# Moving the expert-part table comparisons from VectorE to GpSimd, with the row-0 cases gathered in a tile of their own

## The chip, the cores and the metric

The kernel runs on one core of a Trainium2 chip. The metric is the device time of one execution in microseconds (us), lower is better. The engines are TensorE (PE; its weight loads are PEld), VectorE (DVE), ScalarE (ACT), GpSimd (POOL) and SyncE (SP), which here only issues DMAs.

## The reference

Two layers act on the same normalised input and are added to it (S = 2048 tokens, D = 512):

```python
xn = _layernorm(x, axis=-1)
return x + _A_ref(xn, dft_seq_re, dft_seq_im, dft_hid_re, dft_hid_im) + _B_ref(xn, w_q, k1, k2, u, v)
# A: y = Cr @ (xn @ Wr.T) - Ci @ (xn @ Wi.T)          (2048x2048 and 512x512 matrices)
# B: 32 heads; two score sets against 64 keys, the best 2 of each, the best 2 of the 4 sums,
#    softmax over these, then sum over heads and both picks of g * gelu(xn . u[e]) * v[e], 4096 experts
```

The Fourier matrices of A are inputs like any other. The kernel computes A with the symmetries that a Fourier matrix has, from a part of each matrix, and so has to find out whether the matrices that it was given have those symmetries. If one does not, a slower path at the end recomputes A.

## The kernel before, in words

**Stages.** Up to about 80 us the Fourier part of A is done. Up to about 440 us the scores of the 32 heads are computed in eight groups of four heads, and each token's two experts per head are chosen (the routing). The rest, from about 440 us, is the expert part: 14 blocks of 128 tokens run densely over all 4096 experts on TensorE, and the last two blocks (`NS = 2`) run sparsely, by fetching the rows of u and v that their tokens picked.

**A block of the expert part** has 16 steps: eight `v_part` steps (a product with v into the accumulator `pv`, lines 1018 to 1025) and eight `u_part` steps for the block two ahead (lines 947 to 961). In between, `g_mm` builds one-hot matrices on VectorE (L980, L988, L991) and multiplies them on TensorE (L993), `w_part` forms the weights (L1004 on VectorE, L1011 on ScalarE, L1014 on VectorE), and `finish` evicts `pv` with the VectorE instruction L1038. That instruction frees a PSUM buffer which the next `u_part` steps need.

**The sparse rows** run beside the dense blocks. `fetch` gathers one row per token with an indirect DMA from GpSimd (L1049) into one of five `ga` buffers; `dot` multiplies on VectorE (L1065); `gain` scales on ScalarE (L1075, L1076, L1078) and adds into `ov` on GpSimd (L1083), after which the next row is fetched. There are 128 such rounds.

**The comparisons.** `compare(n)` (lines 720 to 788) tests one 128x1024 piece of the sequence matrices, n from 0 to 63: `ri` (real or imaginary) is n // 32, the column group `g` is n // 8 % 4, and `kk` is n % 8. Its two DMAs from SP (L731 from `ca`, 128 rows of 512 bytes, and L732 from `cb`, 128 rows of 3584 bytes) fill a tile `cx`. `diff` replaces three of its four sections by differences (or sums) to the first and folds the first onto itself (`mirror`); `judge` sums the absolute values on ScalarE (L778 what should be zero, L780 the rest). For g = 0 row 0 of the tile has rules of its own, so `diff` uses L739, L741 (twice, with the mask `not0`), L743 and a second `mirror` on row 0 alone; for other groups one or two tensor_tensor instructions (L752) do it. 28 pieces (`EARLY`, 8 to 23 and 40 to 51) are compared in the routing stage, on GpSimd. The other 36 (0 to 7, 24 to 39, 52 to 63) are compared in the expert part, where `at` is None and `v_eng` is VectorE. `compare_w` (lines 1108 to 1144) does the same for the hidden-dimension matrices, on VectorE, in four more units.

**Order.** `paced` hands out one unit of two streams at every step, the `fit` units at even steps and the compare units at odd ones, spread over 12 blocks. `after(2, f)` puts the work two steps later, and the judging two steps after that, and `hold` ties these to the step's last matmul in the scheduler's order. Each engine runs its instructions in the order in which they stand. The tiles of `compare`, of `fit` (512 KB weight pieces read by ScalarE, L1150 and L1151) and of `w_part` share one tag of `WB = 4` buffers, so a load waits until the buffer's last reader is done. All loads named here stand in SP's one queue, with those of the token blocks (L939, L944), of the rows to be added (L1031) and the stores (L1039).

Of the kernel before, what the change touches and what calls it, by code (L numbers as in the profile page):

```python
# [8 lines left out]
F32 = mybir.dt.float32  # L9
# [6 lines left out]
AF = mybir.ActivationFunctionType  # L16
# [3 lines left out]
P = 128  # L20
# [16 lines left out]
def tile_fnet_peer(ctx, tc, x, ca, cb, c5, wt, wf, wr, wq, kt, ut, vn, uv, out):  # L37
# [57 lines left out]
    sums_sb = cst.tile([P, 138 + NF + 3], F32, name="sums")  # L95
    chk, asum = sums_sb[:, 0:70], sums_sb[:, 70:138]
# [5 lines left out]
    fits = sums_sb[:, 138:]  # L102
# [453 lines left out]
    def part_b(safe, stS, stP, stE, xt, u_sb, cmp_p):  # L556
# [163 lines left out]
        def compare(n, at=None):  # L720
# [10 lines left out]
            nc.sync.dma_start(tf[:, :P], ca[ri, g, :, kk * P:(kk + 1) * P])  # L731
            nc.sync.dma_start(tf[:, P:], cb[ri, g, kk].rearrange("p b c -> p (b c)"))  # L732
            sgn = (((1, 1, 1), (-1, 1, -1)), ((-1, -1, 1), (1, -1, -1)))[ri][odd]
            ops = [ALU.subtract if v > 0 else ALU.add for v in sgn]
            op = ops[1]

            def diff():
                if g == 0:
                    nc.vector.tensor_tensor(tv[:, 1], tv[:, 1], tv[:, 0], op=ops[0])  # L739
                    for i in (2, 3):  # L740
                        nc.vector.scalar_tensor_tensor(tv[:, i], tv[:, 0], not0, tv[:, i], op0=ALU.mult, op1=ops[i - 1])  # L741
                    f = (-1 if ri else 1) * sgn[1] * sgn[2]
                    nc.vector.tensor_tensor(tv[0:1, 3], tv[0:1, 3], tv[0:1, 2],  # L743
                                            op=ALU.subtract if f > 0 else ALU.add)
                else:
                    sets = {}
                    for i, o in enumerate(ops):
                        sets.setdefault(o, []).append(i + 1)
                    for o, ix in sets.items():
                        sl = slice(ix[0], ix[-1] + 1, ix[1] - ix[0] if len(ix) > 1 else 1)  # L750
                        v = tv[:, sl]
                        v_eng.tensor_tensor(v, v, tv[:, 0:1].to_broadcast([P, len(ix), 256]), op=o)  # L752
                m = ALU.add if ri else ALU.subtract

                def mirror(v):

                    c = 0 if kk else 1
                    v_eng.tensor_tensor(v[:, 2:4, c:], v[:, 2:4, c:], v[:, 0:2, c:], op=m)  # L758
# [3 lines left out]
                if g == 0:  # L762
# [332 lines left out]
        def pick(after, k=1):  # L1095
            done[0] += k
            made = nc.cur_bb.bb.instructions
            for f in picks[done[1]:-(-len(picks) * done[0] // turns)]:
# [3 lines left out]
                for i in made[first:]:  # L1102
                    if i.engine in (mybir.EngineType.DVE, mybir.EngineType.Activation):
                        follow(i, after)
                    if i.engine == mybir.EngineType.Activation and after.ins.name in GL:
                        follow(i, GL[after.ins.name])

        def compare_w(n):


# [24 lines left out]
                nc.vector.memset(r[:, 255:256], 0.0)  # L1135
            nc.vector.scalar_tensor_tensor(v[2], v[0], not0, v[2], op0=ALU.mult, op1=op)
            if ri:
                nc.scalar.activation(v[0][0:1, 0:P], v[0][0:1, 0:P], AF.Abs, accum_out=chk[0:1, 68 + half:69 + half])
# [5 lines left out]
            after(2, lambda: nc.scalar.activation(f, f, AF.Abs, accum_out=chk[:, n:n + 1]))  # L1144

        def fit(n):

# [14 lines left out]
        def verdict():  # L1162
# [1 line left out]


            N = NF + 3
            fm = sums_sb[:, 138 + NF:]
# [3 lines left out]
            cols = ((slice(0, 64), 50), (slice(64, 70), 47))  # L1171
            for i, (c, k) in enumerate(cols):
                nc.vector.tensor_reduce(fa[:, i:i + 1], asum[:, c.start:min(c.stop, 68)], axis=AX.X, op=ALU.add)
# [6 lines left out]
            k = nc.gpsimd.partition_all_reduce(fr[:, 2:], sums_sb[:, 138:], P, bass_isa.ReduceOp.absmax)  # L1180
# [21 lines left out]
            NW + k, *range(2 * k, min(2 * k + 2, NW)), NW + 16 + k)]  # L1202
        todo_n = [n for n in range(68) if n not in EARLY]
        units = [lambda n=n: (compare if n < 64 else compare_w)(n) for n in todo_n]
        streams = [[fit_units, 0, 0], [units, 0, 0]]

        def flush(mm):
# [11 lines left out]
                st[2] += 1  # L1219

        if not safe:
            nc.vector.memset(chk[:, 68:70], 0.0)
# [237 lines left out]
```

## Time and profile before

| what | value |
|---|---|
| median of 3 runs | 1119.79 us (1116.18 to 1124.1) |
| the profiled execution | 1113.87 us |
| its span, first to last instruction | 1112.1 us |
| busy share of the span | PE 96%, DVE 90%, ACT 65%, POOL 58% |
| DMA traffic | 196.72 MB, mean 177 GB/s |
| mean granted TensorE clock | 0.987 of full speed |

The profiled execution is 5.9 us below the median of the runs. In the views quoted below, a waiting row reads "engine, line, tile waited <- who released it: us in total, times, longest us"; a group row reads "line engine operation out<-in shapes xcount | busy us, mean ns of one | idle time before it and what ended it"; a timeline row begins with start and duration in us; a row of the windows view gives a stretch, its length, each engine's busy us (and its instructions), the granted clock, the mean busy share of the 16 DMA engines and their GB/s.

### The profile page before, as it was taken

Reading aid. Unit: us, or ns where it says so; the run is one execution under the profiler, and the core shown is the slowest. Engines: PE = TensorE matmul, PEld = TensorE weight load, DVE = VectorE, ACT = ScalarE, POOL = GpSimd, SP = SyncE. Lnnn points to the kernel's source line nnn. Section 1 sums busy time; section 2 is a strip of 40 time slices with the busy share of each in tenths; the row PEclk is TensorE's granted clock in tenths of the full one; section 3 lists DMA queues with packets and bytes.
Section 4 is the critical chain, followed back from the end, with each engine's and each line's share of the span. In section 5 each row is a group of like instructions: output and inputs, shape, how many; then the busy total and the mean of one; then the engine's idle time right before and its main releaser. Section 6 shows DMA issues by size and latency. Waiting matters only on the chain. (4 is left out here: it accounts for less than half of the span.)

```text
span 1112.1 us, 28462 instructions
## 1 busy us (share of the span) xinstructions
PE 1070.3 (96%) x11070; PEld 700.6 (63%) x11070; DVE 996.7 (90%) x2786; ACT 717.7 (65%) x1324; POOL 640.3 (58%) x552
## 2 busy tenths in 40 slices
PE   5899999999999999999999999999998999999897
PEld 4355555454544544987695776968667686786853
DVE  6978897978999999987999999999999999998981
ACT  3576657778788767423766667767566666765660
POOL 0013537588797855211668677756666667667651
PEclk9899999999999999999999999999998999999899
DMA  8248153535446332553677577676767567776521
GB/s 326 83 172 284 49 198 113 173 125 198 153 153 206 106 114 65 186 158 109 186 213 238 193 212 231 225 232 201 215 199 209 182 214 237 230 222 189 158 67 51
DMA packets 84433, 196.72 MB, mean 177 GB/s; under 512 B 10294, under 2 KB 27069, under 8 KB 84288
## 3 DMA queue, kind: packets, MB, share of 16 engines
q1 hardware_dynamic: 63394, 123.49, 33.1%
q0 software_dynamic: 20736, 71.31, 21.8%
q8 instruction: 88, 1.44, 0.5%
q14 instruction: 57, 0.47, 0.1%
q10 hardware_dynamic: 158, 0.01, 0.0%
HBM read 177.68 MB, written 17.10 MB: 175 GB/s over the span
## 5 line engine op out<-in xcount | busy, mean ns | idle before, releaser
L796 PE MATMUL s<-m,xq 128*128 128x512 f16 x1536 | 338.9, 379 | 0.0
L956 PE MATMUL z<-xb,u 128*128 128x128 f16 x5376 | 313.9, 221 | 15.5 <-DVE y L1038 15.5
L956 PEld LDWEIGHTS <-u 128*128 128x128 f16 x5376 | 307.6, 99 | 19.2 <-issue 16.4
L1083 POOL TENSOR_TENSOR ov<-ov,ga 128x512 f32<-128x512 f32 x128 | 203.5, 1590 | 167.2 <-ACT ga L1078 145.7
L1023 PE MATMUL v<-v,act 128*128 128x512 f16 x1344 | 298.6, 379 | 0.0
L796 PEld LDWEIGHTS <-xq 128*128 128x128 f16 x1536 | 148.3, 98 | 171.4 <-issue 0.2
L1023 PEld LDWEIGHTS <-act 128*128 128x128 f16 x1344 | 128.3, 98 | 146.1
L1049 POOL DMA_INDIRECT ga<-in_uv_dram,eix x128 | 173.0, 1351 | 47.2 <-POOL ov L1083 34.2
L980 DVE TENSOR_TENSOR L<-io_lam,cmp 128x2048 f16<-128x2048 f16 x112 | 157.8, 1441 | 13.5 <-PE g L993 13.5
L804 DVE MAX8 vals<-ss 128x8 f32<-128x64 f32 x1024 | 152.4, 216 | 14.1 <-ACT ss L801 14.0
L959 ACT ACTIVATE act<-z,scl 128x512 f32<-128x512 f32 x112 | 75.8, 679 | 97.2 <-PE z L956 96.3
L808 DVE FIND_INDEX8 idx<-vals,ss 128x8 uint16<-128x256 f32 x256 | 107.1, 418 | 0.0
L801 ACT ACTIVATE ss<-s,wsc 128x512 f32<-128x512 f32 x112 | 75.5, 680 | 43.4 <-PE s L796 33.7
L1011 ACT ACTIVATE act<-w 128x1024 f16<-128x1024 f32 x56 | 75.5, 1348 | 43.3 <-DVE w L1004 39.8
L1078 ACT ACTIVATE ga<-ga,za 128x512 f32<-128x512 f32 x128 | 92.1, 721 | 9.8 <-ACT za L1076 0.4
L1014 DVE TENSOR_TENSOR act<-w,act 128x1024 f16<-128x1024 f32 x56 | 86.1, 1539 | 6.7 <-ACT act L1011 5.8
L778 ACT ACTIVATE cx<-cx 128x896 f32<-128x896 f32 x64 | 60.6, 946 | 40.3 <-DVE cx L758 12.9
L1065 DVE SCALAR_TENSOR_TENSOR ga<-ga,px 128x512 f32<-128x512 f32 x128 | 85.6, 676 | 0.1
L1004 DVE SCALAR_TENSOR_TENSOR w<-act,scl,g 128x1024 f32<-128x1024 f32 x56 | 70.9, 1271 | 0.4 <-ACT act L959 0.2
L169 POOL TENSOR_TENSOR wq<-wq,wh 128x1024 f16<-128x1024 f32 x26 | 55.4, 2134 | 24.4 <-ACT wq L166 23.7
L993 PEld LDWEIGHTS <-L 128*128 128x128 f16 x1792 | 52.2, 96 | 9.5 <-issue 2.7
L993 PE MATMUL g<-R,L 128*128 128x32 f16 x1792 | 54.0, 176 | 2.2 <-DVE w L1004 1.9
(274 smaller groups left out, 1312.4 us busy)
## 6 DMA issues: line engine op xcount, KB each, us to landing
cx<-in_cb_dram SPq DMA_DIRECT2D x64, 448.0 KB, 4.6
wq<-in_wq_dram SPq DMA_DIRECT2D x32, 512.0 KB, 5.8
fit<-in_wq_dram SPq DMA_DIRECT2D x28, 512.0 KB, 5.4
uv<-in_ut_dram SPq DMA_DIRECT2D x16, 512.0 KB, 4.1
uv<-in_vn_dram SPq DMA_DIRECT2D x16, 512.0 KB, 3.5
xq<-in_x_dram SPq DMA_DIRECT2D x8, 512.0 KB
xt_d<-xq SPq DMA_DIRECT2D x16, 256.0 KB, 3.0
cx<-in_ca_dram SPq DMA_DIRECT2D x64, 64.0 KB, 2.8
```

The source lines that it names most:

```text
L796: mm = nc.tensor.matmul(ps, xt[i][:, l, kd, :], m[:, r, kd, :], start=(n == 0), stop=(n == 3 * KD - 1))
L804: nc.vector.max(vals[:, i, w, :, h], s[:, g, :])
L808: nc.vector.max_index(idx[:, i, w].rearrange("p k h -> p (k h)"), vals[:, i, w, 0:2].rearrange("p k h -> p (k h)"), s[:, w * HC:g + 1, :]. ...
L956: mm = nc.tensor.matmul(p[:, cc * P:(cc + 1) * P], ug[:, l, c % 2, kd, :], xb[:, r, kd, :], start=(n == 0), stop=(n == 3 * KD - 1))
L980: nc.vector.tensor_tensor(L.rearrange("p t (l two) -> p t l two", two=2), io_lam.rearrange("p (l two) -> p l two", two=2).unsqueeze(1).to_ ...
L993: i = nc.tensor.matmul(p[:, hf, t * NC:(t + 1) * NC], L[:, t, :], R[:, hf * 16 + t, :], start=True, stop=True)
L1014: nc.vector.tensor_tensor(w16[..., 1], w, w16[..., 0], op=ALU.subtract)
L1023: mm = nc.tensor.matmul(pv, w16[:, c, :, l], vg[:, r, c % 2, :], start=(c == 0 and k == 0), stop=(c == NC - 1 and k == 2))
L1049: nc.gpsimd.indirect_dma_start(out=t, out_offset=None, in_=uv, in_offset=bass.IndirectOffsetOnAxis(ap=eix[:, n].rearrange("p k h -> p (k h ...
L1065: nc.vector.scalar_tensor_tensor(t, t, 1.0, T["x"], op0=ALU.mult, op1=ALU.mult, accum_out=T["z", n][:, s:s + 1])
L1078: nc.scalar.activation(t, t, AF.Copy, scale=z)
L1083: T["a"] = nc.gpsimd.tensor_tensor(o, o, t, op=ALU.add)
```

## The change

All compares of the expert part but two (n = 0 and 32, that is g = 0 with kk = 0) run on GpSimd. For the 14 others with g = 0 the rules for row 0 are taken out: rows 1 to 127 are loaded as before, and row 0 of the tile is filled with row 1 once more, by DMAs of one row, so that the form of the other groups serves. Row 0 of these 14 pieces goes into one extra tile `cx_r` (new function `compare_r`): three or four rows in each of four partition quadrants, one class of signs each, compared on VectorE and summed by one ScalarE instruction. The tile is cleared on GpSimd before its eight DMAs. `compare_r` is put in as the third unit of the compare stream, which then has 41 units, and the column sums get one column more.

```diff
-            v_eng = nc.vector if at is None else nc.gpsimd
+            v_eng = nc.vector if n % 32 == 0 else nc.gpsimd
...
-            nc.sync.dma_start(tf[:, :P], ca[ri, g, :, kk * P:(kk + 1) * P])
-            nc.sync.dma_start(tf[:, P:], cb[ri, g, kk].rearrange("p b c -> p (b c)"))
+            own = g == 0 and kk == 0
+            two = ((slice(1, P), slice(1, P)), (slice(0, 1), slice(1, 2)))
+            for e, a in two if g == 0 and kk else ((slice(0, P),) * 2,):
+                nc.sync.dma_start(tf[e, :P], ca[ri, g, a, kk * P:(kk + 1) * P])
+                nc.sync.dma_start(tf[e, P:], cb[ri, g, kk, a].rearrange("p b c -> p (b c)"))
...
-                if g == 0:
+                if own:
                     nc.vector.tensor_tensor(tv[:, 1], tv[:, 1], tv[:, 0], op=ops[0])
...
+        def compare_r(n):
+            t = bp.tile([P, 4, 4, 64], F32, tag="w", name="cx_r", bufs=WB)
+            nc.gpsimd.memset(tf, 0.0)
+            for c in range(4):
+                ri, odd = divmod(c, 2)
+                k0, k1 = (4, 8) if odd else (1, 4)
+                e = slice(32 * c, 32 * c + k1 - k0)
+                nc.sync.dma_start(tf[e, :P], ca[ri, 0, 0:1, k0 * P:k1 * P].rearrange("o (k f) -> (o k) f", f=P))
+                nc.sync.dma_start(tf[e, P:], cb[ri, 0, k0:k1, 0:1].rearrange("k o b c -> (k o) (b c)"))
+            def work():
+                for ri, odd, e in cls:
+                    nc.vector.tensor_tensor(tv[e, 1], tv[e, 1], tv[e, 0], op=ALU.subtract if sgn[0] > 0 else ALU.add)
+                    nc.vector.tensor_tensor(tv[e, 3], tv[e, 3], tv[e, 2], op=ALU.subtract if f > 0 else ALU.add)
+                    nc.vector.tensor_tensor(t[e, 0::2, 2:4], t[e, 0::2, 2:4], t[e, 0::2, 0:2], op=m)
...
+        units.insert(2, lambda: compare_r(64))
```

How this moves instructions is shown at three places. A number at the end of a tile's name only tells its allocation; cx3, cx4, cx5 are the tiles of compare(3), compare(4), compare(5). Lines from 738 on have moved down by 3, so that L1038 is L1041 after the change, L1065 is L1068, L980 is L983, L1004 is L1007.

VectorE, from the third token block's one-hot matrices L to the eviction of its `pv` (tile y2), before, where cx6 is compared:

```order
L980 TENSOR_TENSOR L0_5792<-io_lam_72,cmp4_8578 128x2048
L980 TENSOR_TENSOR L1_5793<-io_lam_72,cmp4_8578 128x2048
L739 TENSOR_TENSOR cx6_8610<-cx6_8610 128x256
L741 SCALAR_TENSOR_TENSOR cx6_8610<-cx6_8610,not0_87 128x256 x2
L1065 SCALAR_TENSOR_TENSOR ga0_22_8542,za0_7124<-ga0_22_8542,px0_7123 128x512
L743 TENSOR_TENSOR cx6_8610<-cx6_8610 1x256
L758 TENSOR_TENSOR cx6_8610<-cx6_8610 128x128
L758 TENSOR_TENSOR cx6_8610<-cx6_8610 1x128
L1038 SCALAR_TENSOR_TENSOR y2_8586<-v2_8444,scl_101,y2_8586 128x512
```

The same place on VectorE after the change:

```order
L983 TENSOR_TENSOR L0_5792<-io_lam_72,cmp4_8587 128x2048
L983 TENSOR_TENSOR L1_5793<-io_lam_72,cmp4_8587 128x2048
L1068 SCALAR_TENSOR_TENSOR ga0_22_8546,za0_7124<-ga0_22_8546,px0_7123 128x512
L1041 SCALAR_TENSOR_TENSOR y2_8595<-v2_8451,scl_101,y2_8595 128x512
L1007 SCALAR_TENSOR_TENSOR w3_3_8966<-act3_7789,scl_101,g3_3_8640 128x1024
```

No compare stands ahead of this eviction any more.

GpSimd near the same place, after the change; before, the L1083 and L1049 pairs (here L1086 and L1052) follow each other with nothing between:

```order
L1086 TENSOR_TENSOR ov0_7195<-ov0_7195,ga0_15_7963 128x512
L1052 DMA ga0_20_8449<-in_uv_dram,eix_99 128x1024
L755 TENSOR_TENSOR cx4_8439<-cx4_8439 128x2x256
L755 TENSOR_TENSOR cx4_8439<-cx4_8439 128x256
L761 TENSOR_TENSOR cx4_8439<-cx4_8439 128x128
L1086 TENSOR_TENSOR ov0_7195<-ov0_7195,ga0_16_8024 128x512
L1052 DMA ga0_21_8490<-in_uv_dram,eix_99 128x1024
```

The additions and gathers of the sparse rows now stand behind the compare, and behind its wait for the load.

SP, where the tile of compare(3) is loaded, before:

```order
L731 DMA cx3_7886<-in_ca_dram 128x128
L732 DMA cx3_7886<-in_cb_dram 128x896
L1150 DMA fit3_8104<-in_wq_dram 128x1024
L1039 DMA out_0_dram<-y1_7789 128x512
L1031 DMA y2_8586<-y_d_57 128x512
```

And on SP after the change, from compare(3) on:

```order
L734 DMA cx3_8168<-in_ca_dram 127x128
L735 DMA cx3_8168<-in_cb_dram 127x896
L734 DMA cx3_8168<-in_ca_dram 1x128
L735 DMA cx3_8168<-in_cb_dram 1x896
L734 DMA cx4_8439<-in_ca_dram 127x128
L735 DMA cx4_8439<-in_cb_dram 127x896
L734 DMA cx4_8439<-in_ca_dram 1x128
L735 DMA cx4_8439<-in_cb_dram 1x896
L942 DMA xb_4_8582<-xt_d_58 128x1024
```

A load of 128 rows has become one of 127 rows and one of a single row, twice per tile, and the other loads stand behind these.

More of the change, by code (lines that the diff above doesn't have):

```diff
@@ L94, in tile_fnet_peer @@
     early = cst.tile([P, len(EARLY)], F32, name="early")
-    sums_sb = cst.tile([P, 138 + NF + 3], F32, name="sums")
-    chk, asum = sums_sb[:, 0:70], sums_sb[:, 70:138]
+    sums_sb = cst.tile([P, 139 + NF + 3], F32, name="sums")
+    chk, asum = sums_sb[:, 0:71], sums_sb[:, 71:139]
     wsc = cst.tile([P, 5], F32, name="wsc")
@@ L1106, in pick @@
                         follow(i, GL[after.ins.name])
+        def compare_r(n):
+            t = bp.tile([P, 4, 4, 64], F32, tag="w", name="cx_r", bufs=WB)
+            tf = t.rearrange("p s q c -> p (s q c)")
+            tv = t.rearrange("p s q c -> p s (q c)")
+            nc.gpsimd.memset(tf, 0.0)
+            cls = []
+            for c in range(4):
[4 more added lines that the diff above has]
+                nc.sync.dma_start(tf[e, P:], cb[ri, 0, k0:k1, 0:1].rearrange("k o b c -> (k o) (b c)"))
+                cls.append((ri, odd, e))
+            def work():
+                for ri, odd, e in cls:
+                    sgn = (((1, 1, 1), (-1, 1, -1)), ((-1, -1, 1), (1, -1, -1)))[ri][odd]
+                    f = (-1 if ri else 1) * sgn[1] * sgn[2]
+                    m = ALU.add if ri else ALU.subtract
+                    nc.vector.tensor_tensor(tv[e, 1], tv[e, 1], tv[e, 0], op=ALU.subtract if sgn[0] > 0 else ALU.add)
+                    nc.vector.tensor_tensor(tv[e, 3], tv[e, 3], tv[e, 2], op=ALU.subtract if f > 0 else ALU.add)
+                    nc.vector.tensor_tensor(t[e, 0::2, 2:4], t[e, 0::2, 2:4], t[e, 0::2, 0:2], op=m)
+                    if odd and ri:
+                        nc.vector.tensor_copy(t[e, 2, 0:2], t[e, 0, 0:2])
+                    elif odd == ri:
+                        nc.vector.memset(t[e, 2, 0:2], 0.0)
+                after(2, lambda: nc.scalar.activation(tf[:, P:], tf[:, P:], AF.Abs, accum_out=chk[:, n:n + 1]))
+            after(2, work)
         def compare_w(n):
@@ L1170, in verdict @@
             o = bp.tile([1, 8], F32, tag="ok", name="ok", bufs=1)
-            cols = ((slice(0, 64), 50), (slice(64, 70), 47))
-            for i, (c, k) in enumerate(cols):
-                nc.vector.tensor_reduce(fa[:, i:i + 1], asum[:, c.start:min(c.stop, 68)], axis=AX.X, op=ALU.add)
+            cols = ((slice(0, 65), 50), (slice(65, 71), 47))
+            for i, c in enumerate((slice(0, 64), slice(64, 68))):
+                nc.vector.tensor_reduce(fa[:, i:i + 1], asum[:, c], axis=AX.X, op=ALU.add)
             nc.vector.tensor_scalar(bnd, bnd, -31.5, None, op0=ALU.add)
```

14 lines of the change are left out of this document (7 added, 7 removed).

## The prediction

> **What bounds the kernel now.** I read the page's busy shares first, then who waited for whom on TensorE, then the instructions around one such wait, then the expert part by windows.
>
> ```profile
> PE 1070.3 (96%) x11070; PEld 700.6 (63%) x11070; DVE 996.7 (90%) x2786; ACT 717.7 (65%) x1324; POOL 640.3 (58%) x552
> ...
> PE z L956 <- DVE y L1038: 15.5, 6, 4.8
> PE g L993 <- DVE w L1004: 1.9, 1, 1.9
> ...
> 607.98 1.50 DVE L739 TENSOR_TENSOR cx<-cx 128x256 f32<-128x256 f32 x1
> 609.40 0.91 DVE L741 SCALAR_TENSOR_TENSOR cx<-cx,not 128x256 f32<-128x256 f32 x2
> ...
> 612.66 0.73 DVE L1038 SCALAR_TENSOR_TENSOR y<-v,scl,y 128x512 f32<-128x512 f32 x1
> ...
> 613.45 0.72 PE L956 MATMUL z<-xb,u 128*128 128x128 f16 x10 [2.71 <-DVE y L1038]
> ...
> 520.00:1040.00 520.00, 504.51 (x6702) 378.88 (x6699) 500.73 (x700) 354.19 (x758) 354.61 (x249) 0.99 0.68 212
> 800.00:900.00 100.00, 95.33 (x1229) 72.24 (x1227) 95.41 (x130) 64.51 (x140) 66.33 (x47) 0.95 0.67 204
> ```
>
> TensorE is the bound. What it loses in the expert part is 15.5 + 1.9 = 17.4 us of waits, nearly all for the eviction L1038, which comes late because VectorE (500.7 of 520 us busy) has work queued ahead of it; at 612.66 us that work is a compare with g = 0. A stretch with such waits also shows a lower clock (0.95 from 800 to 900 us, some 5 us). So relieving VectorE is worth at most some 22 us. The DMA engines are busy 0.68 of this stage, GpSimd 354.6 of 520 us.
>
> **The change, VectorE and GpSimd.** The compares on VectorE, the same instructions where GpSimd runs them in the routing stage, and one VectorE instruction with two SBUF inputs:
>
> ```profile
> L752 DVE TENSOR_TENSOR cx<-cx 128x512 f32<-128x512 f32 (+2 forms) x36 | 31.2, 902 | 3.5 <-DMA cx<-in_cb_dram 3.5
> L758 DVE TENSOR_TENSOR cx<-cx 128x128 f32<-128x128 f32 (+3 forms) x52 | 29.6, 592 | 0.1
> L741 DVE SCALAR_TENSOR_TENSOR cx<-cx,not 128x256 f32<-128x256 f32 x32 | 19.8, 659 | 0.0
> L739 DVE TENSOR_TENSOR cx<-cx 128x256 f32<-128x256 f32 x16 | 12.5, 781 | 0.0
> L743 DVE TENSOR_TENSOR cx<-cx 1x256 f32<-1x256 f32 x16 | 10.0, 623 | 0.0
> ...
> L752 POOL TENSOR_TENSOR cx<-cx 128x512 f32<-128x512 f32 x20 | 25.5, 1274 | 2.8 <-DMA cx<-in_cb_dram 2.8
> L752 POOL TENSOR_TENSOR cx<-cx 128x256 f32<-128x256 f32 x20 | 14.7, 734 | 0.0
> L752 POOL TENSOR_TENSOR cx<-cx 128x768 f32<-128x768 f32 x8 | 14.6, 1822 | 0.0
> L758 POOL TENSOR_TENSOR cx<-cx 128x128 f32<-128x128 f32 x24 | 10.9, 456 | 8.2 <-issue 6.9
> ...
> L980 DVE TENSOR_TENSOR L<-io_lam,cmp x88: 1198/1212/2876, 522.0 to 1031.9; 128x2048 f16<-128x2048 f16 x88
> ...
> POOL ov L1083 <- ACT ga L1078: 145.7, 52, 22.1
> ```
>
> VectorE loses 103 us of rows less about 9 for the two units that stay: 94 us. Of the 34 moved units 7 take 1.82 + 0.46 us on GpSimd and 27 take 1.27 + 0.73 + 0.46: 7 x 2.28 + 27 x 2.46 = 82 us. Added on VectorE is `compare_r`, 14 small instructions at about the 0.4 us of a short one, 6 us once; its ScalarE sum is one more beside 36, its eight loads move 3 or 4 rows each and its clearing on GpSimd is about a microsecond. I cost these at 0 to 3 us, covered by the 145.7 us in which GpSimd waits for ScalarE and by the 94 us freed.
>
> GpSimd's work disturbs VectorE: L980 takes 1.2 us in most cases and up to 2.88. [...] Between nothing and 82 us I take half of the moved time, so VectorE is relieved by some 45 us over 11 blocks, 4 us a block, enough for waits of at most 4.8 us. With nothing else in the change, 12 of the 17.4 us and the 5 us of clock would go.
>
> **The change, the loads.** The 14 units with g = 0 no longer load 128 rows but 127 and 1. Where does the kernel before move 127 rows? Twice, and the trace shows what it costs:
>
> ```profile
> 16.97 0.30 SPq L277 DMA_DIRECT2D c<-in_ca_dram  x1
> 18.31 13.82 SPq L278 DMA_DIRECT2D c<-in_ca_dram  x1
> ...
> 26.00:33.00 7.00, 4.12 (x11) 2.05 (x10) 7.00 (x25) 4.00 (x9) 0.00 (x0) 0.67 0.06 26
> ...
> 121.38 0.22 SPq L547 DMA_DIRECT2D y_d<-u  x1
> 121.69 0.93 SPq L546 DMA_DIRECT2D y_d<-u  x1
> 122.71 0.35 SPq L548 DMA_DIRECT2D y_d<-u  x1
> 124.37 5.71 SPq L547 DMA_DIRECT2D y_d<-u  x1
> 130.17 5.25 SPq L546 DMA_DIRECT2D y_d<-u  x1
> ...
> 130.00:135.00 5.00, 5.00 (x25) 2.29 (x24) 4.70 (x13) 4.98 (x10) 4.32 (x5) 1.00 0.08 29
> ...
> cx<-in_cb_dram SPq DMA_DIRECT2D x64, 448.0 KB, 4.6
> ```
>
> L277 loads 127 rows of 4096 bytes. While it drains, from 26 to 33 us, the 16 DMA engines are busy 0.06, one sixteenth, and move 26 GB/s: one engine works through the whole transfer, and SP's next DMA, of a single row, takes 13.82 us to issue. L547 and L548 store rows 1 to 127 of a tile (`r = slice(1, P)`): again a share of 0.08 and 29 GB/s, and SP stuck for 5.71 and 5.25 us. The transfers that L548 and L547 left there came one after the other, although issued together: had they run on different engines the share would have been 0.12.
>
> [...]
>
> One load is 127 x (512 + 3584) = 520,192 bytes; at 26 GB/s that is 20.0 us, in place of 1.3 us on each of 16 engines. Who stands behind it, and how close the units follow, is in these rows:
>
> ```profile
> L778 ACT ACTIVATE cx<-cx x36: 922/949/952, 531.1 to 1014.9; 128x896 f32<-128x896 f32 x36
> ...
> 657.65 0.37 SPq L731 DMA_DIRECT2D cx<-in_ca_dram  x1
> 658.08 0.44 SPq L732 DMA_DIRECT2D cx<-in_cb_dram  x1
> ...
> q1 hardware_dynamic: 63394, 123.49, 33.1%
> q0 software_dynamic: 20736, 71.31, 21.8%
> ```
>
> 36 judgements between 531.1 and 1014.9 us are one unit every 13.8 us. (40 units are spread over the 94 odd steps of 12 blocks, one in 4.7 steps of both kinds, so a step is 13.8 / 4.7 = 2.9, some 3 us.) In that time this one engine must also carry its share of everything else: 0.68 x 13.8 = 9.4 us less the 1.3 us replaced, 8.1 us (by bytes, 212 / 16 = 13.3 GB/s at 26, only 7.0 - 1.3 = 5.7). So a unit needs 28.1 us of the engine where TensorE gives it 13.8. It cannot hide: a tile is judged four steps of 3 us after its load, the compare's wait stands on GpSimd ahead of the additions and gathers of the sparse rows, the judge on ScalarE ahead of the z evictions, and the tile holds one of four buffers that the weights of `w_part` need. Weight pieces, token blocks and rows that SP loads behind it have a share on the same engine and come late too.
>
> Low end: 25.7 us a unit, 11.9 too many, x 14 = 167 us, less 17 us of running ahead at each of the two groups of seven units: +133. High end, each load beginning when the tile before it is free: 20.0 us stretched by the gathers, which have 21.8 of 54.9 of the traffic and so 0.27 of an engine, is 27.4; from issue to landing 3.5 more (the 4.6 of now less 1.1 for 8 rows of 3584 bytes at 26 GB/s), issue 0.37 + 0.44 = 0.8, GpSimd 2.5, ScalarE 1.1: 35.3 us, 21.5 too many, x 14 = +301. Most of these tiles take the buffer of a weight piece or of a `w` tile and not that of the compare before, so I take a third of the way from the 28.1 of a busy engine to 35.3: 30.5 us, 16.7 too many, x 14 = 234, less 12 us of lead (four steps) for each group, 210. Of the gain above I keep 10 us, for the stretches with g of 2 and 3.
>
> Sum: 1112.1 + 210 - 10 = 1312 us of span; the profiled execution lies 1.8 us above its span, so 1314; the median of the runs shown lies 5.9 us above the profiled one, so 1320.
>
> **The rivals.** First, the loads are in time after all, because a contiguous source is spread over more engines or the lead covers it. Then the first part alone counts: 1112 - 17 + 2 = 1097 us, and 1103 with the 5.9. The 508 KB that kept one sixteenth busy are contiguous in memory too, which speaks against it. This is the one on the other side; it decides if the 127-row load lands within some 12 us, four steps.
>
> Second, the engine's queue is late but the kernel absorbs more: GpSimd, ScalarE and SP have idle time, and if only the first load of each group and a few us of each other show (5 us a unit), it is 1112 + 14 x 5 + 8 = 1190. For it speaks ScalarE's idle third; against it the order, in which all three engines wait in line.
>
> [...]
>
> That the change does nothing can be excluded: the orders show the compares gone from VectorE and the row counts changed.
>
> **How the numbers follow.** A measurement of this kernel can tell about 1% from no change. The load-bound case has 0.79 and by its two ends reaches from 1112 + 133 - 10 + 8 = 1243 to 1112 + 301 + 8 = 1421. The second rival has 0.12, the first 0.06, the third 0.03, of which 0.02 within 1%. The range of eight in ten runs from 1200 to 1420, taking in the upper part of the second rival. Faster by over 1%: 0.06; within 1%: 0.02; slower: 0.92. [...]
>
> **What would show it.** Right: the 127-row loads of `cx` land after 20 us or more; SP is stuck for several us at DMAs behind them; the waits of GpSimd's L755 and of ScalarE's judge and L1151 (now L1185) on DMA are long in two groups, early in the expert part and about its middle; the DMA share falls well below 0.68 there; and TensorE waits there. The compares of groups 2 and 3 on GpSimd should be smooth, with few waits of z for the eviction. [...]

## The result, and the profile after the change

| what | before | after |
|---|---|---|
| median of the runs | 1121.94 us (1116.18 to 1129.47, 4 runs) | 1334.89 us (1330.57 to 1336.05, 4 runs) |
| ratio to before | 1 | 1.1886, 95% interval 1.1807 to 1.1966 |
| span of the profiled execution | 1112.1 us | 1332.1 us |
| TensorE idle in that span | 41.8 us (1112.1 - 1070.3) | 222.6 us (1332.1 - 1109.5) |
| mean granted TensorE clock | 0.987 | 0.914 |

The change makes the kernel 19% slower. The page of the profile after it, its busy line:

```profile
PE 1109.5 (83%) x11070; PEld 725.5 (54%) x11070; DVE 945.2 (71%) x2649; ACT 717.2 (54%) x1326; POOL 715.6 (54%) x652
```

VectorE is down by 51.5 us and GpSimd up by 75.3, the directions that the change intends. TensorE runs the same 11070 matmuls and is busy 39.2 us longer with them, and idle 180.8 us longer: together the 220.0 us of the span. Who waits for whom, from 500 us to the end:

```profile
POOL cx L755 <- DMA cx<-in_cb_dram: 216.8, 13, 20.9
ACT cx L781 <- POOL cx L761: 208.8, 23, 23.3
...
ACT fit L1185 <- DMA fit<-in_wq_dram: 89.7, 6, 21.3
DVE R L991 <- ACT cmp L699: 83.3, 11, 20.2
...
DVE ga L1068 <- DMA ga<-in_uv_dram,eix: 59.9, 9, 22.5
PE z L959 <- DVE y L1041: 58.5, 8, 23.3
```

Read it from above, as a chain. GpSimd waits 13 times, some 17 us each, for a load of `cx`. ScalarE's judge waits for GpSimd. Behind the judge stand the instructions for which VectorE and in the end TensorE wait. The weight pieces (`fit`) and the gathered rows (`ga`), which the change doesn't touch, are late by the same 20 us. The windows of the kernel after, each row a stretch with its engines' busy us, the granted clock, the DMA engines' busy share and their GB/s:

```profile
600.00:700.00 100.00, 63.78 (x753) 50.53 (x753) 45.83 (x59) 39.82 (x86) 41.17 (x34) 0.79 0.35 104
...
800.00:900.00 100.00, 94.84 (x1231) 70.77 (x1229) 74.41 (x93) 57.51 (x122) 66.00 (x55) 0.98 0.55 174
900.00:1000.00 100.00, 45.46 (x574) 34.79 (x575) 37.05 (x48) 29.22 (x66) 34.49 (x32) 0.69 0.35 108
1000.00:1100.00 100.00, 60.69 (x646) 43.76 (x645) 45.48 (x55) 39.62 (x88) 52.53 (x43) 0.78 0.42 127
1100.00:1200.00 100.00, 96.49 (x1264) 72.58 (x1263) 85.21 (x95) 66.80 (x142) 86.84 (x69) 0.97 0.68 207
```

The loss lies in two places, around 650 and around 1000 us: these are the two groups of seven pieces whose loads were changed. Between and behind them TensorE is the bound again at 94.84 and 96.49 of 100 us. In the two places no engine is busy for more than 64 of 100 us and the DMA share has fallen to 0.35 (0.42 from 1000 to 1100 us): nothing is short but one thing that the mean hides. One such load, on SP's timeline, on GpSimd's, and in a short window in which little else moves:

```profile
564.28 2.82 SPq L735 DMA_DIRECT2D cx<-in_cb_dram  x1
567.15 13.48 SPq L734 DMA_DIRECT2D cx<-in_ca_dram  x1
...
616.38 11.58 SPq L735 DMA_DIRECT2D cx<-in_cb_dram  x1
628.00 11.56 SPq L734 DMA_DIRECT2D cx<-in_ca_dram  x1
```

```profile
595.08 1.80 POOL L755 TENSOR_TENSOR cx<-cx 128x768 f32<-128x768 f32 x1 [20.88 <-DMA cx<-in_cb_dram]
```

```profile
615.00:627.00 12.00, 12.00 (x86) 5.90 (x84) 1.66 (x3) 0.00 (x0) 0.00 (x0) 1.00 0.07 27
```

The load of 127 rows is issued at 564.28; its compare starts at 595.08, 30.8 us later. SP is stuck for 13.48 us at the DMA of a single row behind it. While such a load drains, one sixteenth of the DMA engines is busy (0.07) and 27 GB/s move.

How much each group costs is read from the starts of the judge on ScalarE. Here are those of n = 0, 7, 32 and 39, before, and then after:

```profile
531.14 0.94 ACT L778 ACTIVATE cx<-cx 128x896 f32<-128x896 f32 x1
626.60 0.95 ACT L778 ACTIVATE cx<-cx 128x896 f32<-128x896 f32 x1 [0.74 <-DVE cx L758]
745.11 0.95 ACT L778 ACTIVATE cx<-cx 128x896 f32<-128x896 f32 x1 [4.37 <-DVE cx L773]
850.83 0.95 ACT L778 ACTIVATE cx<-cx 128x896 f32<-128x896 f32 x1 [4.37 <-DVE cx L766]
```

```profile
531.82 0.94 ACT L781 ACTIVATE cx<-cx 128x896 f32<-128x896 f32 x1
744.12 0.95 ACT L781 ACTIVATE cx<-cx 128x896 f32<-128x896 f32 x1 [21.41 <-POOL cx L761]
859.48 0.95 ACT L781 ACTIVATE cx<-cx 128x896 f32<-128x896 f32 x1 [1.13 <-DVE cx L776]
1072.79 0.95 ACT L781 ACTIVATE cx<-cx 128x896 f32<-128x896 f32 x1 [13.46 <-POOL cx L761]
```

The stretch with the first seven changed pieces takes 212.3 us and took 95.5, that with the second seven 213.3 and 105.7: +116.8 and +107.6. The nine steps between the groups take 115.4 us and took 118.5. So the loss falls on these two stretches. Not all of it need be the loads: the first stretch also holds the unit of the row tile, which the kernel before doesn't have. The kernel with the change but without its loads (an experiment below) has the same units, and its judges of n = 0, 7, 32 and 39 start here:

```profile
533.72 0.94 ACT L780 ACTIVATE cx<-cx 128x896 f32<-128x896 f32 x1
648.79 1.04 ACT L780 ACTIVATE cx<-cx,not 128x896 f32<-128x896 f32 x1 [3.01 <-POOL cx L760]
766.62 0.95 ACT L780 ACTIVATE cx<-cx 128x896 f32<-128x896 f32 x1 [1.12 <-DVE cx L775]
873.86 1.04 ACT L780 ACTIVATE cx<-cx,not 128x896 f32<-128x896 f32 x1 [2.50 <-POOL cx L760]
```

That is 115.1 and 107.2 us, so the loads make 97.2 and 106.1 us of the loss, 203 together. A unit takes 26.5 us in the first stretch (eight units) and 30.5 in the second (seven).

### The profile page after: what moved, and what is told of

Same layout as the page of the kernel before. It is cut to its first block, busy times and chain, and to the rows that moved or that the text cites. A ratio compares the mean times of both kernels' runs of the same rounds, so it can differ in the third digit from the quotient of the medians.

```text
span 1332.1 us, 28514 instructions
## 1 busy us (share of the span) xinstructions
PE 1109.5 (83%) x11070; PEld 725.5 (54%) x11070; DVE 945.2 (71%) x2649; ACT 717.2 (54%) x1326; POOL 715.6 (54%) x652
## 5 line engine op out<-in xcount | busy, mean ns | idle before, releaser
L959 PE MATMUL z<-xb,u 128*128 128x128 f16 x5376 | 336.3, 228 | 129.7 <-DVE y L1041 58.5
L959 PEld LDWEIGHTS <-u 128*128 128x128 f16 x5376 | 328.6, 103 | 135.6 <-issue 124.5
L1026 PE MATMUL v<-v,act 128*128 128x512 f16 x1344 | 311.6, 391 | 0.0
L755 POOL TENSOR_TENSOR cx<-cx 128x512 f32<-128x512 f32 (+2 forms) x109 | 128.1, 1191 | 232.2 <-DMA cx<-in_cb_dram 217.5
L1086 POOL TENSOR_TENSOR ov<-ov,ga 128x512 f32<-128x512 f32 x128 | 185.1, 1446 | 77.6 <-ACT ga L1081 61.4
L1026 PEld LDWEIGHTS <-act 128*128 128x128 f16 x1344 | 131.5, 100 | 155.6 <-issue 16.8
L1052 POOL DMA_INDIRECT ga<-in_uv_dram,eix x128 | 167.7, 1310 | 45.5 <-POOL ov L1086 33.9
L983 DVE TENSOR_TENSOR L<-io_lam,cmp 128x2048 f16<-128x2048 f16 x112 | 159.9, 1464 | 18.1 <-PE g L996 18.1
L1017 DVE TENSOR_TENSOR act<-w,act 128x1024 f16<-128x1024 f32 x56 | 101.7, 1817 | 60.4 <-ACT act L1014 57.6
L1068 DVE SCALAR_TENSOR_TENSOR ga<-ga,px 128x512 f32<-128x512 f32 x128 | 85.9, 680 | 60.1 <-DMA ga<-in_uv_dram,eix 59.9
L991 DVE TENSOR_TENSOR R<-io_c,cmp 128x1024 f16<-128x1024 f16 x56 | 55.1, 984 | 83.3 <-ACT cmp L699 83.3
L1007 DVE SCALAR_TENSOR_TENSOR w<-act,scl,g 128x1024 f32<-128x1024 f32 x56 | 71.2, 1274 | 57.6 <-ACT za L1078 28.2
```

The lines of the kernel that those rows point to most:

```text
L959: mm = nc.tensor.matmul(p[:, cc * P:(cc + 1) * P], ug[:, l, c % 2, kd, :], xb[:, r, kd, :], start=(n == 0), stop=(n == 3 * KD - 1))
L983: nc.vector.tensor_tensor(L.rearrange("p t (l two) -> p t l two", two=2), io_lam.rearrange("p (l two) -> p l two", two=2).unsqueeze(1).to_ ...
L1017: nc.vector.tensor_tensor(w16[..., 1], w, w16[..., 0], op=ALU.subtract)
L1026: mm = nc.tensor.matmul(pv, w16[:, c, :, l], vg[:, r, c % 2, :], start=(c == 0 and k == 0), stop=(c == NC - 1 and k == 2))
L1052: nc.gpsimd.indirect_dma_start(out=t, out_offset=None, in_=uv, in_offset=bass.IndirectOffsetOnAxis(ap=eix[:, n].rearrange("p k h -> p (k h ...
L1086: T["a"] = nc.gpsimd.tensor_tensor(o, o, t, op=ALU.add)
```

## The experiments

Each ratio below is to the kernel before, run beside the experiment on the same chip; it stood at 1118.42 to 1120.56 us there. The rows quoted from the experiments are of the time from 500 us on.

### Is it the loads, and is it one DMA engine?

**126 rows in place of 127.** The changed kernel with

```diff
-            two = ((slice(1, P), slice(1, P)), (slice(0, 1), slice(1, 2)))
+            two = ((slice(1, 127),) * 2, (slice(127, P),) * 2, (slice(0, 1), slice(1, 2)))
```

> The changed kernel, with one edit: each 127-row load of the 14 tiles is split into 126 rows and one row (126 divides by 14, 127 only by 1), so two DMAs more per tile and the same bytes. Theory (the 127-row transfer runs through one DMA engine, and that is the whole loss): the landings come back to about 5 us, the waits of GpSimd's compare and of ScalarE's judge (216.8 and 208.8 us after the change) fall under 20 us, the DMA share from 900 to 1000 us goes back from 0.35 to 0.6 or more, and the time to 1095 to 1115 us. Rival A (the compares on GpSimd, in line ahead of the additions and gathers, or their exclusion with VectorE): unchanged here, so it stays at 1300 us or more. Rival B (the number of DMAs in SP's queue): 28 DMAs more, so slower than the 1335 us of the change.

Measured: 1136.68 us, ratio 1.0149 (1.0121 to 1.0176). One row fewer in the transfer takes away 198 of the 213 us, with two more DMAs per tile. The wait of GpSimd's compare for its load has gone from the list of long waits, and the DMA share from 900 to 1000 us is 0.69. Rivals A and B fall. But the theory's 1095 to 1115 was missed as well: some 16 us stay, and the second part below is about them. ScalarE's judge, too, still waits 83.0 us for GpSimd and not under 20.

**The loads alone.** The kernel before, compares on VectorE as they were, with

```diff
-            nc.sync.dma_start(tf[:, :P], ca[ri, g, :, kk * P:(kk + 1) * P])
-            nc.sync.dma_start(tf[:, P:], cb[ri, g, kk].rearrange("p b c -> p (b c)"))
+            for e in (slice(1, P), slice(0, 1)) if g == 0 and kk and at is None else (slice(0, P),):
+                nc.sync.dma_start(tf[e, :P], ca[ri, g, e, kk * P:(kk + 1) * P])
+                nc.sync.dma_start(tf[e, P:], cb[ri, g, kk, e].rearrange("p b c -> p (b c)"))
```

> The kernel before, compares on VectorE as they were, with only the loads of the 14 tiles split into rows 1 to 127 and row 0. Theory (the loads alone make the loss): VectorE in place of GpSimd waits for the landings, and TensorE behind VectorE even more directly: 1280 to 1380 us. Rival (the loss needs the compare on GpSimd, which holds up the sparse rows while it waits): the wait on VectorE is shorter or covered, under 1200 us. Since VectorE has no idle time to lose (96 percent busy in this stage), a time above the change's 1335 would say that the move to GpSimd even softened the loss.

Measured: 1335.73 us, ratio 1.1916 (1.1884 to 1.1948), the time of the whole change. Here it is VectorE that waits for the load, and GpSimd, which runs no compare, waits behind it. The waits of this kernel from 500 us on:

```profile
POOL ov L1084 <- ACT ga L1079: 368.4, 53, 23.5
DVE cx L740 <- DMA cx<-in_cb_dram: 236.1, 14, 20.9
```

Fourteen waits, one per changed load, up to 20.9 us as after the change. So the compare's place is not needed for the loss: the loads make it.

**The change without its loads.** All 128 rows are loaded by two DMAs as before. Row 0 is kept out of the sum by the mask as ScalarE's scale, and compared in the row tile; compares on GpSimd as in the change:

```diff
-            two = ((slice(1, P), slice(1, P)), (slice(0, 1), slice(1, 2)))
-            for e, a in two if g == 0 and kk else ((slice(0, P),) * 2,):
-                nc.sync.dma_start(tf[e, :P], ca[ri, g, a, kk * P:(kk + 1) * P])
-                nc.sync.dma_start(tf[e, P:], cb[ri, g, kk, a].rearrange("p b c -> p (b c)"))
+            nc.sync.dma_start(tf[:, :P], ca[ri, g, :, kk * P:(kk + 1) * P])
+            nc.sync.dma_start(tf[:, P:], cb[ri, g, kk].rearrange("p b c -> p (b c)"))
+            mask = {"scale": not0} if g == 0 and kk else {}
...
-                nc.scalar.activation(tf[:, P:], tf[:, P:], AF.Abs, accum_out=a[:, k:k + 1])
+                nc.scalar.activation(tf[:, P:], tf[:, P:], AF.Abs, **mask, accum_out=a[:, k:k + 1])
```

> The whole change without its loads: as the experiment with the mask, but with the compares on GpSimd as in the change. The difference to the change is the form of the loads alone, the difference to the mask on VectorE is GpSimd alone. Theory (the loads are about 200 of the 214 us; GpSimd costs rather than gains, as 20 of its pieces cost 4 us): 1124 to 1136 us. Rival, the forecast's own term (10 us of gain from the relief of VectorE): 1105 to 1115 us.

Measured: 1135.03 us, ratio 1.0152 (1.012 to 1.0183). The theory holds: the form of the loads is worth 1334.9 - 1135.0 = 200 us, and the rest of the change costs 1.5% where I had forecast a gain.

**How much by rows.** Two more splits of the 127 rows in the changed kernel:

```diff
-            two = ((slice(1, P), slice(1, P)), (slice(0, 1), slice(1, 2)))
+            two = ((slice(1, 63),) * 2, (slice(63, 125),) * 2, (slice(125, P),) * 2, (slice(0, 1), slice(1, 2)))
```

> The changed kernel with its 127-row loads split into 62, 62 and 3 rows. [...] Theory: that engine then needs 8.1 + 10 = 18.1 us per unit against a pace of 13.8, 4.3 too many, x 14 = 60 less the 17 us of lead for each of two groups, so 1112 + 26 to 60 - 10 + 8: about 1135 to 1170 us, between the first experiment and the change. Rival (each DMA other than a whole 128-row one costs a fixed delay, whatever its rows): six loads per tile and as slow as the change or slower, 1330 us or more. Rival (transfers are not tied to one engine by their row count): as fast as with 126 rows.

and, with 61, 59 and 7 rows,

```diff
-            two = ((slice(1, P), slice(1, P)), (slice(0, 1), slice(1, 2)))
+            two = ((slice(1, 62),) * 2, (slice(62, 121),) * 2, (slice(121, P),) * 2, (slice(0, 1), slice(1, 2)))
```

> The changed kernel with its loads cut into 61, 59 and 7 rows. [...] As many DMAs as with 62, 62 and 3 rows, which took 1195 us. Theory (a transfer on one engine always takes the same one): 61 + 59 + 1 rows of each piece still pass one engine, 121 of 127, so 1290 to 1325 us. Rival (successive transfers take different engines): 61 rows on each of two engines, so as with 62, 62, 3 or better, 1150 to 1205 us.

Measured: 1195.48 us with 62, 62 and 3 rows (ratio 1.0669, 1.0641 to 1.0697), and 1321.58 with 61, 59 and 7 (1.1805, 1.1767 to 1.1843). The first is above its 1135 to 1170, the second within its 1290 to 1325. The 1195.48 lie 58.8 us above the version with 126 rows, about the 60 us that the expectation had without any lead; it was missed because it started from a base that gains 10 us. The 10 us per tile in that sum, half of the 20.0, was an estimate of mine: over how many engines a load of 62 rows is spread, no run shows. Measured is that the waits of GpSimd's compare for its load are 53.9 us in 11 waits there, the longest 10.1, where the change has 216.8 in 13 and 20.9. Both kernels issue the same number of DMAs for the same rows, and differ by 126 us: both rivals of the first fall, and the one of the second.

One rival to the shared engine is left: SP's queue might work its transfers one after the other, whichever engines they use. The trace of the changed kernel decides it. Two weight pieces of 512 KB are issued at 581.83, behind the load of 127 rows that was issued at 564.28 and whose compare starts at 595.08:

```profile
581.83 0.95 SPq L1184 DMA_DIRECT2D fit<-in_wq_dram  x2
...
583.00:586.00 3.00, 3.00 (x31) 3.00 (x30) 1.05 (x2) 0.00 (x0) 0.00 (x0) 0.50 0.97 337
587.00:594.00 7.00, 3.98 (x89) 3.86 (x87) 0.00 (x0) 0.00 (x0) 0.00 (x0) 0.97 0.08 29
594.00:597.00 3.00, 0.00 (x0) 0.00 (x0) 0.00 (x0) 1.02 (x2) 1.84 (x2) 0.50 0.06 26
...
595.98 1.06 ACT L1185 ACTIVATE fit<-fit 128x1024 f32<-128x1024 f32 x1 [16.36 <-DMA fit<-in_wq_dram]
```

From 583 to 586 us, with the 127 rows still under way, nearly all DMA engines are busy (0.97): the queue does move transfers side by side. Then about one sixteenth is busy again, and ScalarE gets the weight piece only at 595.98, when the 127 rows are through. So what is late is the part of it that stands on the same engine. In the kernel with 61 and 59 rows a stretch with little else in it reads:

```profile
610.00:625.00 15.00, 15.00 (x114) 7.78 (x111) 4.46 (x8) 0.69 (x1) 0.00 (x0) 1.00 0.08 28
```

Two loads side by side on two engines would make a share of 0.12. At 0.08 the 61 and the 59 rows don't run side by side here, they share one engine, and 28 GB/s move, as with the 127 rows (0.07 and 27).

The times, and the waits of GpSimd's compare for its load, go with the way the rows of a tile are cut (for the first two kernels the wait is GpSimd's whole idle time ahead of these compares):

| rows of a tile's transfers | compare waits for its load, us | us |
|---|---|---|
| 128 (mask, GpSimd) | 0.5 | 1135.0 |
| 126 + 1 + 1 | 0.6 | 1136.7 |
| 62 + 62 + 3 + 1 | 53.9 | 1195.5 |
| 61 + 59 + 7 + 1 | 191.4 | 1321.6 |
| 127 + 1 | 216.8 | 1334.9 |

A row is 4096 bytes, at the 26 GB/s of the kernel before's 127-row load 0.158 us, and 14 tiles make that 2.2 us. By this estimate the 13.3 us between the last two are 6 rows fewer on the busy engine, which leaves 122 of 128: the 61, the 59 and 2 of the other 8. The 139.4 us between 62 + 62 + 3 + 1 and 127 + 1 are 63 rows, half of a tile. The 198.2 us between 126 + 1 + 1 and 127 + 1 are 90, so up to some 38 rows of a tile the engine's load is hidden, if the line stays straight (no run lies between the second and the third of the table). The prediction's own terms give about the same point: 13.8 us of pace less 8.1 us of other traffic is 5.7 us, or 36 rows. Only for the 127 rows and for the 61 and 59 does a share of the DMA engines show the one engine.

### What does the move to GpSimd do by itself?

**Only the other groups' compares on GpSimd.** The kernel before with

```diff
-            v_eng = nc.vector if at is None else nc.gpsimd
+            v_eng = nc.vector if g == 0 else nc.gpsimd
```

> The kernel before, with only the 20 pieces of the other column groups (24 to 31, 52 to 63) compared on GpSimd; all loads are of 128 rows and the 16 pieces of the first group stay on VectorE. [...] Theory: VectorE loses some 45 us of rows, the waits of TensorE for the eviction shrink in that half of the part: 1105 to 1117 us where the kernel before has 1119 to 1122, a gain of 0 to 1.3 percent. [...] Rival (GpSimd's line delays the sparse rows, and they the end): waits of TensorE appear for tiles of the sparse rows at the end of the kernel.

Measured: 1124.24 us, ratio 1.0042 (1.0025 to 1.006): above the theory's 1105 to 1117, and the one-hot instruction goes from 1474 to 1594 ns. GpSimd is busy 50.9 us more (640.3 to 691.2), VectorE only 5.9 us less (996.7 to 990.8), although the compares of 20 pieces left it. TensorE waits for the eviction more, not less:

```profile
PE z L956 <- DVE y L1038: 23.5, 8, 7.0
```

**All compares back on VectorE**, in the kernel with 126-row loads:

```diff
-            v_eng = nc.vector if n % 32 == 0 else nc.gpsimd
+            v_eng = nc.vector if at is None else nc.gpsimd
```

> The first experiment (126-row loads, row-0 tile, plain form) with the compares of the expert part back on VectorE. The first experiment stood at 1136.7 us, 16 above the kernel before. Theory A (the rest of the loss is GpSimd: its work and VectorE's two-input instructions exclude each other, and its line delays the judges): 1105 to 1122 us, and the sum of waits of TensorE for the eviction falls back from 25.4 to about 15 us. Theory B (the rest of the loss is the loads: six DMAs in place of two, on 14 engines and one): it stays at 1130 to 1140 us.

Measured: 1109.88 us, ratio 0.9906 (0.9878 to 0.9934), theory A; TensorE's waits for the eviction fall to 8.3 us, below the 15 expected. This is faster than both kernels of this study, by 0.9% against the kernel before. How much of that is the simpler form for the first column group is taken up at the end. Against it, the same kernel with the compares on GpSimd (1136.68) loses 27 us. The one-hot instruction, the largest group of VectorE, in the version on VectorE and then in that on GpSimd:

```profile
L983 DVE TENSOR_TENSOR L<-io_lam,cmp 128x2048 f16<-128x2048 f16 x98 | 133.9, 1404 | 15.4 <-PE g L996 15.3
...
L1017 DVE TENSOR_TENSOR act<-w,act 128x1024 f16<-128x1024 f32 x52 | 74.7, 1438 | 10.0 <-ACT act L1014 8.6 <-ACT za L1078 1.4
...
L1007 DVE SCALAR_TENSOR_TENSOR w<-act,scl,g 128x1024 f32<-128x1024 f32 x50 | 63.5, 1274 | 0.4 <-PE g L996 0.2
```

```profile
L983 DVE TENSOR_TENSOR L<-io_lam,cmp 128x2048 f16<-128x2048 f16 x98 | 154.2, 1610 | 14.3 <-PE g L996 14.2
L1017 DVE TENSOR_TENSOR act<-w,act 128x1024 f16<-128x1024 f32 x52 | 98.2, 1889 | 13.5 <-ACT act L1014 10.7 <-ACT za L1078 2.8
...
L1007 DVE SCALAR_TENSOR_TENSOR w<-act,scl,g 128x1024 f32<-128x1024 f32 x51 | 64.8, 1273 | 7.6 <-ACT za L1078 2.7 <-issue 1.7 <-ACT act L962 1.7
```

L983, with both inputs in SBUF, goes from 1404 to 1610 ns, and L1017 goes from 1438 to 1889. L1007, whose input g lies in PSUM, stays at 1274 and 1273.

**The plain form with the mask, on VectorE.** The kernel of the change without its loads, with the same edit of `v_eng`:

> The plain form for the 14 pieces with no change of their loads: all 128 rows are loaded by two DMAs as before, the sum of absolute values takes row 0 times zero (the mask as the scale of ScalarE's instruction), row 0 is compared in the row tile as in the change, and all compares stay on VectorE. VectorE loses some 1.2 us per piece of its special rules and gains 6 once. Theory (the loads made the loss, GpSimd the small rest, the plain form itself is good): 1108 to 1120 us, equal to the kernel before or up to 1 percent faster. Rival (the row tile with its eight DMAs and its clearing costs something by itself): 1122 to 1130.

Measured: 1123.16 us, ratio 1.0039 (1.0022 to 1.0056). By the number that is the rival, a cost of the row tile; but the 126-row version has the same row tile and is 13 us faster, so the row tile isn't it. GpSimd against VectorE with the mask is 1135.03 to 1123.16, 12 us, where with 126-row loads it was 27.

**Work on GpSimd that nobody needs.** On the 1109.88 us version, in `gain`, ahead of each of the 128 additions:

```diff
...
-            for t in T.pop("t"):
+            for ga, t in T.pop("t"):
+                nc.gpsimd.tensor_tensor(ga[:, :256], ga[:, :256], ga[:, 256:D], op=ALU.add)
```

> The version with 126-row loads and all compares on VectorE (1109.9 us), with work added on GpSimd that nobody needs: before each of the 128 additions of a sparse row, one tensor_tensor of 128x256 on the dead half of that row's buffer. At 0.73 us each that is some 93 us of GpSimd work with two SBUF inputs, about what the moved compares take there (99 us from 634.4 to 734.0); VectorE and ScalarE keep their order word for word. Theory (GpSimd's reading of SBUF stretches VectorE's two-input instructions): 1122 to 1140 us, and the 128x2048 one-hot instruction, 1412 ns in the mean over 94, goes above 1550. Rival (what cost time with the compares on GpSimd was the judges that wait behind them in GpSimd's line): nobody waits for this work, so 1108 to 1115 us.

and its twin, which only writes:

```diff
...
-            for t in T.pop("t"):
+            for ga, t in T.pop("t"):
+                nc.gpsimd.memset(ga[:, :D], 0.0)
+                nc.gpsimd.memset(ga[:, :256], 0.0)
```

> The twin of the experiment with the added tensor_tensor: at the same places GpSimd clears the dead half with two memsets (128x512 and 128x256, estimated at 0.97 us x 768 / 1024 = 0.73 us together from the one memset of 128x1024 in the trace), which write but read nothing. VectorE and ScalarE again keep their order. Theory (it is the reading that excludes): 1108 to 1116 us, VectorE's instructions not stretched more than with no added work. Rival (any GpSimd work disturbs, or the sparse rows come late behind it): as slow as with the tensor_tensor.

Measured: 1158.65 us with the tensor_tensor (ratio 1.0357, 1.0321 to 1.0392) and 1109.29 with the memsets (0.9919, 0.989 to 0.9949). The added groups on GpSimd, and the one-hot instruction beside them, first in the kernel with the tensor_tensor, then in the twin:

```profile
L983 DVE TENSOR_TENSOR L<-io_lam,cmp 128x2048 f16<-128x2048 f16 x98 | 153.2, 1601 | 6.3 <-PE g L996 6.1
...
L1087 POOL TENSOR_TENSOR ga<-ga 128x256 f32<-128x256 f32 x128 | 147.3, 1157 | 69.0 <-DVE ga L1068 65.5 <-DVE cx L1169 1.9
```

```profile
L983 DVE TENSOR_TENSOR L<-io_lam,cmp 128x2048 f16<-128x2048 f16 x98 | 134.3, 1406 | 8.2 <-PE g L996 7.7 <-issue 0.3
...
L1087 POOL MEMSET ga<- 128x512 f32 x128 | 71.1, 556 | 48.5 <-DVE ga L1068 48.3
L1088 POOL MEMSET ga<- 128x256 f32 x128 | 40.8, 319 | 5.7
```

111.9 us of clearing cost nothing, and the one-hot instruction stays at 1406 ns. 147.3 us of adding cost 49 us (1158.65 - 1109.88), and it goes to 1601, while the added instruction itself takes 1157 ns where I had counted 0.73 us. Nobody waits for the result of either, and the sparse rows stand behind both alike. VectorE is busy for 1046.9 us with the tensor_tensor, 977.0 with the memsets and 975.4 with neither, and TensorE's waits for the eviction follow it, first with the tensor_tensor, then in the twin:

```profile
PE z L959 <- DVE y L1041: 35.2, 10, 7.4
```

```profile
PE z L959 <- DVE y L1041: 6.8, 2, 3.8
```

So for this work it isn't the place in GpSimd's line that costs, it is that GpSimd reads SBUF (the tensor_tensor, L983 at 1601 ns) and doesn't only write there (the memsets, 1406), while VectorE reads two inputs there. Whether one SBUF input on GpSimd would be enough was not tried. For the moved compares the place in line isn't excluded as a second part: ScalarE's judges wait 83.0 us for them in the kernel with 126-row loads, and VectorE's one-hot instruction L991 then waits 20.1 us for ScalarE's cmp, where it waits 9.1 with the compares on VectorE.

### What stays open

**The row tile late**, on the 1109.88 us version:

```diff
-        units.insert(2, lambda: compare_r(64))
+        units.insert(36, lambda: compare_r(64))
```

> The version with 126-row loads on VectorE (1109.9 us), with the row-0 tile as the 37th unit of the compare stream instead of the third. Early, its 14 small instructions stand in the VectorE-bound start, late in a stretch where VectorE has 20 to 25 of 100 us free. Expected: 1104 to 1112 us; if the version's gain came from a lucky order of a few VectorE instructions and not from fewer of them, it moves by up to 1 percent in either direction, as the version with the mask did (1123).

Measured: 1115.59 us, ratio 0.9971 (0.9948 to 0.9994), outside its 1104 to 1112: a loss of 6 us, within the 1% named for a lucky order.

**The mask added to the 126-row version on VectorE**, the same scale on ScalarE's sum as above:

> The version with 126-row loads on VectorE with the mask added as the scale of ScalarE's sums, that is the mask version with the other loads. Its VectorE order is word for word that of the 126-row version. Theory (the 13 us between the two versions, 1109.9 and 1123.2, come from the order of some VectorE instructions, a compare ahead of the first eviction in the mask version, and not from the mask): 1107 to 1113. Rival (the scaled sum on ScalarE is slower): 1120 to 1125.

Measured: 1116.29 us, ratio 0.997 (0.9947 to 0.9993): neither 1107 to 1113 nor 1120 to 1125. The masked sum itself takes longer by little:

```profile
L782 ACT ACTIVATE cx<-cx 128x896 f32<-128x896 f32 x22 | 20.6, 938 | 6.2 <-DVE cx L762 4.7 <-DVE cx L777 1.2
L782 ACT ACTIVATE cx<-cx,not 128x896 f32<-128x896 f32 x14 | 14.5, 1037 | 17.0 <-DVE cx L762 17.0
```

0.1 us 14 times is 1.4 us, not the 6.4 between the two versions. Why small edits that leave VectorE's order alone, or move some instructions of it, shift this kernel by half a percent isn't settled here. So the 0.9% of the 126-row version is measured, but how much of it is fewer VectorE instructions and how much the fall of their order is open.

## Why the prediction was right, point by point

**The bound** was named rightly: outside the two groups TensorE is back at 94.84 and 96.49 of 100 us, and the only stretches that lost are those where a load is waited for.

**The loads**, forecast at +210 us, cost some 200 us (the change against the change without its loads) to 215 us (the loads alone against the kernel before). The step held in its mechanism: one engine at 26 GB/s (27 in a quiet window), the same one each time (a share of 0.08 with 61 + 59 rows). In the two stretches the loads make 203 us, where 16.7 x 14 = 234 less 24 of lead had been counted. A unit every 30.5 us is what the second stretch has; in the first it is 26.5. The plain 28.1 us of a busy engine per unit gives (28.1 - 13.8) x 14 = 200 as well. The two corrections to it, 2.4 us more per unit (34 us in all) and 24 us of lead, nearly cancel, and no run tests either alone. The 1.3 us on each of 16 engines, which the sum took off for the load replaced, no run shows for a load of `cx`: its 448 KB landed in 4.6 us before, and after the change the share was 0.97 while two weight pieces of 128 rows moved.

**The gain from VectorE's relief**, -10 us, is the step that failed. "Between nothing and 82 us I take half of the moved time": with loads of 126 rows the moved compares take 111.6 us on GpSimd (27 x (1.453 + 1.049 + 0.919) + 7 x (1.824 + 0.919)) and not 82, stretched as the added tensor_tensor above was. VectorE is relieved by 28.1 us (996.7 to 968.6) and not by 45, and 21.3 of these come with the plain form alone, the compares still on VectorE (975.4): the move itself relieves it by 6.8. The half of the moved time was an estimate of mine that no run shows; in place of its 45 us the runs showed these 6.8. And what is left on it is late at the wrong places: TensorE's waits for the eviction rise from 15.5 us to the 25.4 of the kernel with 126-row loads,

```profile
PE z L959 <- DVE y L1041: 25.4, 8, 6.8
```

So the change without its loads is worth +16 us (1.5%). The third case, with 0.03, in which GpSimd takes back on VectorE what the move frees, was right for this part of the change: it stands at 1135 us with harmless loads. In the sum it is 26 us too few here (-10 in place of +16) and 10 too many for the loads (210 in place of 200), which is about the 15 us between 1320 and 1334.9: two errors of opposite sign partly cancel in the total, which is luck. The parts don't simply add, though: on top of the loads the move cost nothing (1334.9 against 1335.7 for the loads alone), perhaps because VectorE waits in the two groups anyway, which was not tested.

**The first and second rivals** fall with the first load quoted above: its compare starts 30.8 us after the issue, so it does not land within 12 us. And of each load not 5 us show but some 14 (200 / 14); about 5.7 us are absorbed.

**What the prediction did not have** is TensorE's clock. It is granted 0.79 and 0.69 in the groups, and the same matmuls take 39.2 us longer. The sum went by the pace of the units and so came out without it; a sum of waits would have been 39 us short.

## What to carry to other kernels

Look at the row count of every transfer that a change touches, before its bytes: here one row cut off 128 turned a load that landed in 4.6 us into one for which its compare waited up to 20.9 us, and no busy share shows it, since the mean over the 16 DMA engines went down, from 0.71 to 0.35 between 600 and 700 us. Work moved to an engine with idle time wasn't free here where it read the same memory (147.3 us of adding on GpSimd cost 49 us, 111.9 us of clearing nothing): compare the stretched and the unstretched duration of the instructions that stay, before the move is counted as relief. Where a transfer must lose a row, measure other ways to cut it (126 and one in place of 127 took 198 us off), or load all rows and mask in the sum, which took 200 us off.

## What the runs showed of the hardware

- A 127-row load holds up SP's queue too: the next DMAs took 13.48, 11.58 and 11.56 us to issue, where the two DMAs of a tile took 0.37 and 0.44 before the change. ScalarE waited up to 21.3 us for 512 KB loads issued behind it (16.36 for the one shown above).
- GpSimd's memset, 111.9 us of it, did not slow VectorE's one-hot instruction (1404 and 1406 ns); GpSimd's tensor_tensor, 147.3 us, did (1601 ns), and was itself stretched to 1157 ns. A VectorE instruction with one input in PSUM (L1007) was stretched by neither: 1271 ns beside the memset, 1273 beside the tensor_tensor, 1274 without them.
- With the same 11070 matmuls, the granted clock fell to 0.69 from 900 to 1000 us, a stretch with many waits, and stood at 0.97 and 0.98 in the two stretches where TensorE was busy for 94 us and more of 100.
